# Cosine attention and a gated MLP in one kernel: loads, engine orders and the last store rearranged

## The chip, the cores and the metric

The kernel runs on one core of a Trainium2 chip. The metric is device time in microseconds (us) of one execution. A core has five engines that run at the same time, each with its own in-order list of instructions: TensorE (PE; its weight loads are shown as PEld), VectorE (DVE), ScalarE (ACT), GpSimd (POOL) and SyncE (SP). SP, ACT and POOL also issue DMA transfers from their lists. An instruction that waits for a semaphore holds back everything behind it on its engine.

## What is computed

For 8 batches of 12 heads (448 positions, 64 wide): rows of q and k are divided by their norms, the scores divided by tau = 0.1, softmax over the keys, and the product with v. The 12 heads' results side by side are the 3584 x 768 input of an MLP with 2048 hidden columns:

```python
q_n = q / (norm(q) + 1e-06);  k_n = k / (norm(k) + 1e-06)
scores = q_n @ k_n.T / tau
attn = exp(scores - max);  attn = attn / (sum(attn) + 1e-09)
x = (attn @ v)  # 12 heads side by side: [3584, 768]
h = x @ w_in
out = (h * cos(h)) @ w_out
```

## The kernel before

**Tiles.** Two pairs of heads make a "quad": 24 quads, three to a batch. A quad's Q and K (448 KB each) come through the SP queue (`load_one`, L394) into rings of three buffers Qf and Kf; its V comes through the POOL queue (`load_v`, L408) into a ring of four. W1 (the first MLP weight) is loaded in four pieces (`load_w1`, L416), W2 in four chunks (`load_w2`, L424), both on the POOL queue.

**A quad's work.** `square` (L434) squares Q and K on ScalarE or GpSimd, its `add` (L450) sums the squares on VectorE into n2; `inverse` (L458) makes 1/norm: a logarithm and an exponential on ScalarE, a sum with 1e-6 and a reciprocal on VectorE (quad 0: four ScalarE steps). `scale` (L489) multiplies, on VectorE or GpSimd, into Qn and Kn. They are transposed to qT and kT: quads 0 to 3 on TensorE (`transpose`, L510) with a copy from PSUM, later quads by DMA on the SP queue (`turn`, L527). `scores` (L539) is four matmuls into a pair of PSUM banks and one exponential E on ScalarE (L556), seven per quad; `attend` (L559) multiplies E with V. The softmax sums are made by matmuls with ones (`spread`, L579: quads 0 to 5; sums are inverted on ScalarE, L601 and L605) or with a selector (`sums` and `invert`, L622 and L638: later quads; a small store to DRAM from the ACT queue and a broadcast load R on the SP queue). The result goes into xT, by VectorE (L614, L617) or GpSimd (L657).

**The MLP.** For each batch c, a first stage of eight pairs of 12 matmuls (`m1_part`, L669, shown as L675), each pair followed on ScalarE and VectorE by four steps (`m1`: L688, L690, L692, L694) into gT; PSUM banks of a pair are reused after its L694. The second stage (`m2`, L697, shown as L703) makes 128 x 384 halves of a tile t of the output; a copy to osb (L711) follows on VectorE, and after the second half two stores of 64 rows on the SP queue (L717). `fill` cuts the second stage in pieces, and the lists VISITS and LATER (L723, L734) say how many of its matmuls stand between groups of three scores of the next batch's quads.

**Order.** A planner (L22) records operations with a cost and their dependencies. TensorE keeps the order of recording. Up to the line `P.strict = False` (L944) ScalarE, VectorE and GpSimd keep it too, through `behind` (L51); POOL's DMAs always do. After that, and for SP throughout, the planner picks by readiness and urgency in its own time model. So the start of the kernel (quads 0 to 2 and the norms of 3 and 4, L803 to L945) is an order written by hand. There, `gate` (L807) is the loads of quad 1: the first W1 piece waits for them. Quad 5's load waits for W2's chunk 2 (`half[3][:1]`, L895), quad 4's `turn` and quad 6's load for chunks 2 and 3. The copies of quad 3's transposes stand in the first MLP stage (L966).

Of the kernel before, what the change touches and what calls it, by code (L numbers as in the profile page):

```python
# [16 lines left out]
class Op:  # L17
    __slots__ = ("i", "eng", "dur", "fn", "reads", "writes", "deps", "dma", "lat", "start", "end",
                 "count", "waits", "known", "prio", "moves", "mode", "chain", "behind", "lead", "packet", "lock")


class Planner:  # L22
# [20 lines left out]
    def op(self, eng, dur, fn, r=(), w=(), after=(), dma=None, moves=0, mode="f", chain=None, keep=False, lead=0.0,  # L43
           packet=74, lock=False):
        o = Op()
        o.i, o.eng, o.dur, o.fn, o.dma, o.moves, o.mode, o.chain = (
            len(self.ops), eng, dur, fn, dma, moves, mode, chain)
        o.lat = self.FIRST + moves + self.LAST if dma else self.LAT[eng]
        o.behind, o.lead, o.packet, o.lock = None, lead, packet, lock
        if keep or self.strict and eng in ("act", "dve", "pool"):  # L50
            o.behind, self.tail[eng] = self.tail.get(eng), o  # L51
        o.reads, o.writes = tuple(r), tuple(w)
        deps = {a.i for a in after if a is not None}
        for x in o.reads:
            if x in self.last_write:
                deps.add(self.last_write[x].i)
        for x in o.writes:
            if x in self.last_write:
                deps.add(self.last_write[x].i)
            deps.update(p.i for p in self.readers.get(x, ()))  # L60
        deps.discard(o.i)
        o.deps = sorted(deps)
        for x in o.reads:
            self.readers.setdefault(x, []).append(o)
        for x in o.writes:
            self.last_write[x] = o
            self.readers[x] = []
        self.ops.append(o)
        return o
# [11 lines left out]

    PASSES, SPREAD = 0, 1.5

    def plan(self):

        rng = random.Random(1)
        shift = [0.0] * len(self.ops)
        least = max(o.end for o in self.pass_(shift))
        for _ in range(self.PASSES):
            n = rng.choice((8, 30, 100))  # L90
            i = rng.randrange(len(shift) - n)
            tried = list(shift)
            for k in range(i, i + n):
                tried[k] += rng.gauss(0.0, self.SPREAD)
            end = max(o.end for o in self.pass_(tried))
            if end <= least:
                least, shift = end, tried
        self.order = self.pass_(shift)
        return self.order

    def pass_(self, shift):
# [11 lines left out]
        t, urge = 0.0, [1e9] * len(ops)  # L113
        for o in ops:
            if o.eng == "pe":
                urge[o.i] = t
                t += o.dur
        later = None
        behind = {}
        for o in reversed(ops):  # L120
            if o.eng == "pe":
                if later is not None:
                    urge[o.i] = min(urge[o.i], urge[later.i] - o.dur)
                later = o
            if o.chain:
# [7 lines left out]
        for o in ops:  # L133
            o.prio = (urge[o.i] if urge[o.i] < 1e8 else 2000.0 + o.i) + shift[o.i] - o.lead
        pe = [o.i for o in ops if o.eng == "pe"]
        pe_next = 0
# [138 lines left out]
def bass_cosine_attention__then__act_gcu_kernel(  # L275
# [42 lines left out]
    sqk = sb("sqk", [128, 2 * NJ, D], BF16)  # L318
    n2 = ring("n2", 2, [128, 4 * NJ], F32)
    nrm = ring("nrm", 2, [128, 4 * NJ], F32)  # L320
    rr = ring("rr", 2, [128, 4 * NJ], F32)
    ne = ring("ne", 2, [128, 4 * NJ, 2], F32)
    Qn = ring("Qn", 1, [128, NJ, 2, D], BF16)
# [38 lines left out]
    for i in range(2):  # L362
        op("dve", 0.1, lambda e, i=i: e.memset(ne[i].ap()[:, :, 1], 1e-6), w=[("eps", i)])

# [65 lines left out]

    def jr(t, w, part, off=0):
        return bass.AP(t, off + w * H + part[0], [[2 * H, 128], [NJ, 2], [1, part[1] - part[0]]])

    def square(qd, w, eng, part=ALL[0], after=()):  # L434
# [15 lines left out]
        def add():  # L450
            return op("dve", 0.07 + 0.95 * n, lambda e: e.tensor_reduce(  # L451
                out=n2[u].ap()[:, H * w:H * w + H] if part == ALL[0] else jr(n2[u], w, part),
                in_=dst, axis=AX.X, op=ALU.add),
# [4 lines left out]
    def inverse(qd, w0, w1, part=ALL[0], after=()):  # L458
# [5 lines left out]
        if part == ALL[0]:  # L464
            n = slice(H * w0, H * w1)
            t, z, o = n2[u].ap()[:, n], nrm[u].ap()[:, n], rr[u].ap()[:, n]
        else:
            t, z, o = (jr(a[u], w0, part) for a in (n2, nrm, rr))
        act("exp", 0.12, lambda e: e.activation(z, t, ACT.Ln, bias=1e-30, scale=1.0),
# [3 lines left out]
        if qd == 0:  # L473
# [5 lines left out]
            return  # L479
        two_ = ne[u].ap()[:, H * w0:H * w1]  # L480
        act("exp", 0.12, lambda e: e.activation(two_[:, :, 0], z, ACT.Exp, bias=0.0, scale=0.5), r=x, w=[("ne", u)],
# [5 lines left out]
        op("dve", 0.3, lambda e: e.reciprocal(o, z), r=x, w=y, lead=lead)  # L487

    def scale(qd, w, eng="pool", part=ALL[0]):  # L489
        s, u = qd % 3, qd % 2  # L490
        j0, j1 = part
        f, n, nm = ((Qf, Qn, "Q"), (Kf, Kn, "K"))[w]
        rb = bass.AP(rr[u], w * H + j0, [[2 * H, 128], [NJ, 2], [1, j1 - j0], [0, D]])
        return op(eng, (1.05 if eng == "dve" else 1.65) * (j1 - j0) / NJ,
# [14 lines left out]

    def transpose(qd, which, bk, part=ALL[0]):  # L510
        u = qd % 3
# [3 lines left out]
        def mm(e):  # L515
# [122 lines left out]
    def invert(quads, bk):  # L638
# [8 lines left out]
        act("exp", 0.47, lambda e: e.activation(zz, zz, ACT.Exp, bias=0.0, scale=-1.0), r=[("Zs", z)], w=[("Zs", z)], lead=LEAD)  # L647
        op("act", 0.3, lambda e: e.dma_start(rscr.ap()[8 * n:8 * n + rows, :], Zs[z].ap()[0:32 * np_:16, :]),
           r=[("Zs", z)], w=[("rs", n)], dma=("rs", z), moves=0.05, lead=LEAD)
        for i, qd in enumerate(quads):  # L650
            u, sl, b = qd % 2, qd % NA, qd // QB
            for r in range(2):
                ap = bass.AP(rscr, (8 * n + 4 * i + 2 * r) * S, [[0, 64], [S, 2], [1, S]])
                op("sp", 0.6, lambda e, r=r, u=u, ap=ap: e.dma_start(R[u].ap()[64 * r:64 * r + 64], ap),
                   r=[("rs", n)], w=[("R", u, r)], dma=("R", u, r), moves=0.85, packet=140, lead=LEAD)
            c0 = 2 * (qd % QB)
# [40 lines left out]
    def m2(t, h, f0, f1, bk):  # L697
# [11 lines left out]
        if f1 == NNB:  # L709
            so = t % 3  # L710
            op("dve", 0.475, lambda e: e.tensor_copy(osb[so].ap()[:, HW * h:HW * h + HW], bank(bk, HW)),  # L711
               r=whole(bk), w=[("o", so, h)])
            if h:
                for sg in range(2):
                    b, cc = divmod(128 * t + 64 * sg, S)
                    dst = bass.AP(out.tensor, (S * b + cc // 64) * KM, [[NJ * KM, 64], [1, KM]])
                    op("sp", 0.6, lambda e, sg=sg, dst=dst: e.dma_start(dst, osb[so].ap()[64 * sg:64 * sg + 64, :]),  # L717
                       r=[("o", so, 0), ("o", so, 1)], w=[("out", t, sg)], dma=("store", so, sg), moves=0.55, packet=121)

# [3 lines left out]
    VISITS = [  # L723
# [7 lines left out]
        [],  # L731
        [],
    ]
    LATER = {19: 3, 10: -1, 18: -2, 5: 3, 4: 1, 17: 4, 7: -1, 21: -2, 22: -1, 15: -2, 9: 1}  # L734
    E1, E2 = NNB - 6, NNB - 4
# [69 lines left out]
    for part in HALVES:  # L805
        load_one(0, 1, part)
    gate = load_qk(1)  # L807
    load_qk(2)
# [25 lines left out]
    adds = [square(1, w, "act") for w in range(2)]  # L834
    adds[0]()
    load_qk(3)
# [3 lines left out]
    transpose(0, 1, 7, HALVES[1])  # L840
    adds[1]()
    for _ in inverse(1, 0, 2):
# [17 lines left out]
    spread(0, 4, 6)  # L860
    addk = square(2, 1, "act")
    addq = square(2, 0, "pool", after=[scaled])
# [85 lines left out]
    for c in range(B):  # L948
# [106 lines left out]
```

## Time and profile before

| what | value |
|---|---|
| median of three runs | 425.24 us (424.66 to 428.72) |
| the profiled execution | 424.88 us, its span 423.0 us |
| granted TensorE clock | 1.00 |
| first MLP stage begins (first L675) | 34.40 us |
| its second stage begins (first L703) | 54.48 us |
| second batch's first stage begins | 88.97 us |
| last copy ends | 419.35 us |

The span runs from the first to the last instruction; the rest of the time lies around it. A row of the timeline reads: start, duration, engine and line, operation, out<-in with shapes, and in brackets how long the engine had been idle and what ended that. Matmuls are pipelined, so TensorE's busy share includes some time that is not work at its peak. DMA issues are listed with the time from issue to landing.

### The profile page before, as it was taken

The numbers are of one execution on the slowest core, as the hardware profiler recorded it, in microseconds if no ns is written. First come the engines' busy times: TensorE is split into PE (matmuls) and PEld (weight loads), VectorE is DVE, ScalarE is ACT, GpSimd is POOL, SyncE is SP. The second block draws the span as 40 slices with busy tenths as digits, with TensorE's granted clock in tenths as the row PEclk, the third lists the DMA queues.
The fourth block names the chain that finished last, engine by engine and source line by source line (L and its number), as shares of the span: only waits on it lengthen the run. The fifth ranks groups of instructions, "written<-read, shape, count | busy, mean of one in ns | idle before, by whom it ended". The sixth has DMA issues, their size and how long they took to land.

```text
span 423.0 us, 8441 instructions
## 1 busy us (share of the span) xinstructions
PE 406.1 (96%) x3586; PEld 212.6 (50%) x3586; DVE 269.5 (64%) x337; ACT 306.3 (72%) x404; POOL 200.9 (47%) x137
## 2 busy tenths in 40 slices
PE   6879998999999999999999999999999999999995
PEld 5345454445544445445555555445554555555563
DVE  5767886879853659733996269824882228736921
ACT  6998689988888977697787677689678656505700
POOL 3566238792387794758628880559213213000000
PEclk9999999999999999999999999999999999999999
DMA  8999997995099969298909990279805523021022
GB/s 272 259 236 209 242 273 165 186 218 135 4 220 227 283 107 251 67 238 212 229 5 211 206 279 2 52 179 177 166 1 82 128 72 92 2 74 39 0 76 74
DMA packets 68230, 62.94 MB, mean 149 GB/s; under 512 B 39961, under 2 KB 60769, under 8 KB 68193
## 3 DMA queue, kind: packets, MB, share of 16 engines
q1 hardware_dynamic: 57808, 50.48, 48.3%
q0 software_dynamic: 10240, 11.80, 16.8%
q8 instruction: 28, 0.46, 0.5%
q10 hardware_dynamic: 144, 0.13, 0.1%
q14 instruction: 10, 0.07, 0.0%
HBM read 53.87 MB, written 11.14 MB: 154 GB/s over the span
## 4 chain that ended last, share of the span: by engine, by line
PE 77%; DMA 12%; ACT 4%; DVE 3%; POOL 2%; issue 0%; ACTq 0%; SPq 0%
PE PS L703 30%; PE PS L675 30%; PE PS L566 7%; PE PS L549 6%; DMA W<-in_moe_w_out_dram 6%; PE PS L629 3%; DMA Kf<-in_k_dram 3%; ACT E L556 2%; DMA R<-rscr 1%; DVE n L451 1%; PE PS L588 1%; DMA rscr<-Zs 1%; DMA Qf<-in_q_dram 1%; DVE osb L711 1%; POOL xT L657 0%
## 5 line engine op out<-in xcount | busy, mean ns | idle before, releaser
L556 ACT ACTIVATE E<-PS 128x896 bf16<-128x896 f32 x168 | 142.4, 919 | 20.8 <-PE PS L549 18.4
L703 PE MATMUL PS<-W,gT 128*128 128x384 bf16 x896 | 157.0, 327 | 0.0
L675 PE MATMUL PS<-xT,W 128*128 128x448 bf16 x768 | 147.0, 353 | 1.3 <-DVE qT L524 1.0
L703 PEld LDWEIGHTS PS<-W,gT 128*128 128x128 bf16 x896 | 82.9, 98 | 69.8 <-issue 15.9
L675 PEld LDWEIGHTS PS<-xT,W 128*128 128x128 bf16 x768 | 74.7, 98 | 71.7 <-DVE qT L524 1.1
L688 ACT ACTIVATE ar<-PS 128x896 int32<-128x896 f32 x64 | 58.2, 911 | 37.5 <-PE PS L675 37.5
L690 DVE SCALAR_TENSOR_TENSOR ar<-ar,PS 128x896 f32<-128x896 int32 x64 | 69.2, 1083 | 22.3 <-ACT ar L688 22.3
L694 DVE TENSOR_TENSOR gT<-PS,ar 128x896 bf16<-128x896 f32 x64 | 69.5, 1088 | 7.5 <-ACT ar L692 7.1
L692 ACT ACTIVATE ar<-ar 128x896 f32<-128x896 f32 x64 | 60.6, 946 | 18.2 <-DVE ar L690 18.0
L711 DVE COPY osb<-PS 128x384 f32<-128x384 f32 x56 | 31.1, 556 | 61.2 <-PE PS L703 60.5
L657 POOL TENSOR_TENSOR xT<-AVs,R 128x896 bf16<-128x896 f32 x18 | 37.4, 2086 | 49.6 <-DMA R<-rscr 49.6
L549 PE MATMUL PS<-qT,kT 64*64 64x448 bf16 x672 | 49.7, 359 | 5.3 <-ACT E L556 2.8
L447 POOL TENSOR_TENSOR sqq<-Qf 128x896 bf16<-128x896 f32 x22 | 36.9, 1677 | 34.0 <-DVE n L451 14.4
L447 POOL TENSOR_TENSOR sqk<-Kf 128x896 bf16<-128x896 f32 x21 | 36.9, 1756 | 33.2 <-DVE n L451 32.0
L495 POOL TENSOR_TENSOR Qn<-Qf,rr 128x896 bf16<-128x896 f32 x21 | 38.0, 1812 | 24.3 <-DVE rr L487 16.7
L575 DVE COPY AVs<-PS 128x896 f32<-128x896 f32 x21 | 22.8, 1088 | 29.2 <-PE PS L566 29.1
L566 PE MATMUL PS<-E,Vb 64*64 64x448 bf16 x672 | 36.7, 350 | 0.0
L451 DVE TENSOR_REDUCE n<-sqq 128x14 f32<-128x896 bf16 x24 | 25.7, 1072 | 14.3 <-POOL sqq L447 10.2
L549 PEld LDWEIGHTS PS<-qT,kT 64*64 64x64 bf16 x672 | 16.5, 105 | 31.8 <-ACT E L556 12.8
L495 POOL TENSOR_TENSOR Kn<-Kf,rr 128x896 bf16<-128x896 f32 x18 | 30.3, 1685 | 1.8 <-DMA kT<-Kn 1.8
L451 DVE TENSOR_REDUCE n<-sqk 128x14 f32<-128x896 bf16 (+2 forms) x25 | 25.9, 1040 | 5.8 <-POOL sqk L447 5.8
L566 PEld LDWEIGHTS PS<-E,Vb 64*64 64x64 bf16 x672 | 18.8, 107 | 12.7 <-issue 1.9
(45 smaller groups left out, 175.7 us busy)
## 6 DMA issues: line engine op xcount, KB each, us to landing
Qf<-in_q_dram SPq DMA_DIRECT2D x24, 448.0 KB, 5.4
out_dram<-osb SPq DMA_DIRECT2D x56, 192.0 KB, 3.6
Kf<-in_k_dram SPq DMA_DIRECT2D x23, 448.0 KB, 5.9
R<-rscr SPq DMA_DIRECT2D x36, 224.0 KB, 4.5
Vb<-in_v_dram POOLq DMA_DIRECT2D x24, 224.0 KB, 5.7
W<-in_moe_w_in_dram POOLq DMA_DIRECT2D x4, 768.0 KB, 17.7
W<-in_moe_w_out_dram POOLq DMA_DIRECT2D x4, 768.0 KB, 24.4
qT<-Qn SPq DMA_TRANSPOSE x20, 4.1
```

What stands on the lines that cost most here:

```text
L447: op(eng, (1.68 if eng == "pool" else 1.05) * n, lambda e: e.tensor_tensor(dst, src, src, ALU.mult), r=cut(nm + "f", s, part), w=cut("sq" ...
L451: return op("dve", 0.07 + 0.95 * n, lambda e: e.tensor_reduce(out=n2[u].ap()[:, H * w:H * w + H] if part == ALL[0] else jr(n2[u], w, part) ...
L495: lambda e: e.tensor_tensor(n[0].ap()[:, j0:j1].rearrange("p j r d -> p r j d"), f[s].ap()[:, :, j0:j1], rb, ALU.mult),
L549: ins = e.matmul(bank(bs + r, S, 64 * a, 64 * a + 64), kT[u].ap()[64 * r:64 * r + 64, j, a, :], qT[u].ap()[64 * r:64 * r + 64, :, a, :], s ...
L556: act("exp", 0.81, lambda e: e.activation(E[es].ap(), two(bs), ACT.Exp, bias=0.0, scale=INV_TAU), r=pair(bs), w=[("E", es)], chain="E")
L566: ins = e.matmul(bank(bk + a, S, 64 * r, 64 * r + 64), Vb[vs].ap()[64 * a:64 * a + 64, r, j, :], E[es].ap()[64 * a:64 * a + 64, r, :], sta ...
L675: ins = e.matmul(bank(bk + i2), W1.ap()[:, i, 128 * nb:128 * nb + 128], xT[c % 2].ap()[:, i, :], start=(i == 0), stop=(i == NKC - 1))
L688: op("act", 0.815, lambda e: e.activation(ar[s].ap().bitcast(I32), two(bk), ACT.Identity, bias=0.25, scale=INV2PI), r=bs, w=[("ar", s)])
L690: op("dve", 1.005, lambda e: e.scalar_tensor_tensor(ar[s].ap(), ar[s].ap().bitcast(I32), -2.0 * math.pi, two(bk), ALU.mult, ALU.add), r=bs ...
L692: act("sin", 0.86, lambda e: e.activation(ar[s].ap(), ar[s].ap(), ACT.Sin, bias=GUARD * math.pi / 2.0, scale=GUARD), r=[("ar", s)], w=[("a ...
L694: op("dve", 1.01, lambda e: e.tensor_tensor(gT.ap()[:, 2 * pr:2 * pr + 2, col:col + S], two(bk), ar[s].ap(), ALU.mult), r=bs + [("ar", s)] ...
L703: ins = e.matmul(bank(bk, HW), gT.ap()[:, f, col:col + 128], W2.ap()[:, f, HW * h:HW * h + HW], start=(f == 0), stop=(f == NNB - 1))
```

## The change

1. Quad 1's loads wait until quad 0's Q has landed (`load_qk(1, [first])`); quad 2's loads are as before.
2. Each recorded operation gets a key: its number, plus an entry of a table MOVE while `strict` holds. TensorE's list and the strict lists of ScalarE, VectorE, GpSimd and POOL's DMAs are sorted by that key. The random passes of the planner, which were set to none, are gone.
3. The square of quad 2's K moves from ScalarE to GpSimd and is recorded earlier; the squares of quad 1 change places.
4. n2, nrm, rr and ne become one tile each with both buffers; a function `inverse_two` is added, which would make the norms of two quads at once. Nothing calls it.
5. The copies of quad 3's transposes go to ScalarE (`eng="act"`).
6. The planner's costs of the softmax sums' store and broadcast load are raised; VISITS and LATER have new numbers.
7. The last tile's halves are stored each as soon as it is copied, 64 rows from the SP queue and 64 from the ACT queue.

```diff
+        o.key = o.i + (self.MOVE.get(o.i, 0) if self.strict else 0)
         if keep or self.strict and eng in ("act", "dve", "pool"):
-            o.behind, self.tail[eng] = self.tail.get(eng), o
+            self.tail.setdefault(eng, []).append(o)
...
+    MOVE = {50: -10.0, 101: -3.5, 179: -5.0, 83: -3.0, 19: -7.0, 124: -2.5, 94: 0.0, 187: -5.0, 204: 9.0, 123: 9.0,
...
+            140: 5.5, 51: 2.5}
...
+        for line in self.tail.values():
+            line.sort(key=lambda o: o.key)
+            for a, b in zip(line, line[1:]):
+                b.behind = a
...
+        pe = [o.i for o in sorted((o for o in ops if o.eng == "pe"), key=lambda o: o.key)]
...
+        if eng == "act":
+            op("act", 0.13 + 0.067 * (j1 - j0), lambda e: e.activation(dst, src, ACT.Copy), r=whole(bk), w=cut(nm + "T", u, part))
+            return
...
+            if end:
+                store(t, HW * h, HW * h + HW, [("o", so, h)], ("sp", "act"))
+            elif h:
+                store(t, 0, KM, [("o", so, 0), ("o", so, 1)])
...
-        [(0, 25), (3, 12), (3, 11), (3, 6), (3, 0), (3, 10), (3, 12), (3, 5), (3, 5), (3, 0), (3, 4), (3, 4), (1, 1)],
+        [(0, 25), (3, 12), (3, 11), (3, 4), (3, 4), (3, 11), (3, 10), (3, 4), (3, 5), (3, 0), (3, 4), (3, 6), (1, 0)],
...
-    gate = load_qk(1)
+    gate = load_qk(1, [first])
...
     adds = [square(1, w, "act") for w in range(2)]
-    adds[0]()
+    adds[1]()
     load_qk(3)
...
-    adds[1]()
+    adds[0]()
+    addk = square(2, 1, "pool")
...
-    addk = square(2, 1, "act")
...
-                    transpose(FIRST, w, at_bank[pr] + w)
+                    transpose(FIRST, w, at_bank[pr] + w, eng="act")
```

The lists that come of it, up to the first MLP stage, differ in these places (old order, then new):

- SP: Q0, K0, Q1, K1, K2, Q2; now Q0, K0, Q2, K2, (wait for Q0) K1, Q1. Later: quad 7's loads ahead of quad 5's; now quad 5's ahead of quad 7's.
- POOL: V0, V1, two pieces of W1, V2, two of W1, square of quad 2's Q, V3, W2 chunks 0 1 2 3; now V0, V2, V1, three pieces of W1 (first half, second half, first half of the columns), square of quad 2's K, the fourth piece, W2 chunk 2, square of quad 2's Q, chunks 1 3 0, V3.
- ScalarE: the first logarithm of quad 0 ahead of the square of K's second part; quad 1's K squared ahead of its Q; the square of quad 2's K gone; in the first MLP stage the two copies behind L688 of pair 2, and L692 of pair 2 ahead of that of pair 1.
- VectorE: quad 1's sums (K first) ahead of quad 0's last copy; quad 1's last scale ahead of its first copy; quad 2's K sum ahead of quad 1's last copy; quad 2's last copy ahead of quad 0's xT; quad 3's K sum ahead of quad 1's xT; in the first MLP stage the sum of quad 5's Q behind L690 of pair 3 (before: behind the stage).
- TensorE: scores and attends of quads 0 to 2 change places at four points, and five fill-in matmuls stand behind a transpose instead of ahead of it.

More of the change, by code (lines that the diff above doesn't have):

```diff
@@ L18 @@
     __slots__ = ("i", "eng", "dur", "fn", "reads", "writes", "deps", "dma", "lat", "start", "end",
-                 "count", "waits", "known", "prio", "moves", "mode", "chain", "behind", "lead", "packet", "lock")
+                 "count", "waits", "known", "prio", "moves", "mode", "chain", "behind", "lead", "packet", "lock", "key")
 class Planner:
@@ L80, in land @@
         return s + took + self.LAST
-    PASSES, SPREAD = 0, 1.5
-    def plan(self):
[L86 to L98, printed above, removed]
+    MOVE = {50: -10.0, 101: -3.5, 179: -5.0, 83: -3.0, 19: -7.0, 124: -2.5, 94: 0.0, 187: -5.0, 204: 9.0, 123: 9.0,
[7 rows of a table added]
+    def plan(self):
+        for line in self.tail.values():
+            line.sort(key=lambda o: o.key)
+            for a, b in zip(line, line[1:]):
+                b.behind = a
+        self.order = self.pass_([0.0] * len(self.ops))
         return self.order
@@ L113, in pass_ @@
         t, urge = 0.0, [1e9] * len(ops)
[L114 to L118, printed above, removed]
+        pe = [o.i for o in sorted((o for o in ops if o.eng == "pe"), key=lambda o: o.key)]
+        for i in pe:
+            urge[i] = t
+            t += ops[i].dur
+        later = dict(zip(pe, pe[1:]))
         behind = {}
         for o in reversed(ops):
[L121 to L124, printed above, removed]
+            if o.i in later:
+                urge[o.i] = min(urge[o.i], urge[later[o.i]] - o.dur)
             if o.chain:
@@ L134, in pass_ @@
             o.prio = (urge[o.i] if urge[o.i] < 1e8 else 2000.0 + o.i) + shift[o.i] - o.lead
-        pe = [o.i for o in ops if o.eng == "pe"]
         pe_next = 0
@@ L487, in inverse, with inverse_two @@
         op("dve", 0.3, lambda e: e.reciprocal(o, z), r=x, w=y, lead=lead)
+    def inverse_two():
+        flat = "p u n -> p (u n)"
+        t, z, o = (a.ap().rearrange(flat) for a in (n2, nrm, rr))
+        c2, x, y = ([c for u in range(2) for w in range(2) for c in cut("%s%d" % (k, w), u, ALL[0])] for k in ("n2", "nrm", "rr"))
+        both = ne.ap().rearrange("p u n i -> p (u n) i")
+        act("exp", 0.17, lambda e: e.activation(z, t, ACT.Ln, bias=1e-30, scale=1.0), r=c2, w=x)
+        act("exp", 0.17, lambda e: e.activation(both[:, :, 0], z, ACT.Exp, bias=0.0, scale=0.5), r=x,
+            w=[("ne", 0), ("ne", 1)])
+        op("dve", 0.2, lambda e: e.tensor_reduce(out=z, in_=both, axis=AX.X, op=ALU.add),
+           r=[(k, u) for k in ("ne", "eps") for u in range(2)], w=x)
+        op("dve", 0.55, lambda e: e.reciprocal(o, z), r=x, w=y)
     def scale(qd, w, eng="pool", part=ALL[0]):
@@ L508, in norm_b, with transpose @@
         return last
-    def transpose(qd, which, bk, part=ALL[0]):
+    def transpose(qd, which, bk, part=ALL[0], eng="dve"):
         u = qd % 3
@@ L710, in m2, with store @@
             so = t % 3
+            end = t == B * S // 128 - 1
             op("dve", 0.475, lambda e: e.tensor_copy(osb[so].ap()[:, HW * h:HW * h + HW], bank(bk, HW)),
                r=whole(bk), w=[("o", so, h)])
[L713 to L718, printed above, removed]
+            if end:
+                store(t, HW * h, HW * h + HW, [("o", so, h)], ("sp", "act"))
+            elif h:
+                store(t, 0, KM, [("o", so, 0), ("o", so, 1)])
+    def store(t, x0, x1, parts, engs=("sp", "sp")):
+        so = t % 3
+        for sg, eng in enumerate(engs):
+            b, cc = divmod(128 * t + 64 * sg, S)
+            dst = bass.AP(out.tensor, (S * b + cc // 64) * KM + x0, [[NJ * KM, 64], [1, x1 - x0]])
+            src = osb[so].ap()[64 * sg:64 * sg + 64, x0:x1]
+            op(eng, 0.6, lambda e, dst=dst, src=src: e.dma_start(dst, src), r=parts, w=[("out", t, sg, x0)],
+               dma=("store", so, sg, x0), moves=0.55 * (x1 - x0) / KM, packet=121)
     QUADS = [4, 5, 3, 3, 3, 3, 0, 0]
```

32 lines of the change are left out of this document (16 added, 16 removed), and 18 rows, old and new, of tables (MOVE, VISITS).

## The prediction

> **What bounds the kernel now.** I read the page's busy line first, then the chain of waits, then busy time by stretches, then the start and the end of the timeline. TensorE is busy 406.1 of 423.0 us. The chain of waits runs through TensorE almost without a break from 89 us on, and the number of matmuls stays. What can move is the start, the few gaps, and the tail.
>
> ```profile
> PE 406.1 (96%) x3586; PEld 212.6 (50%) x3586; DVE 269.5 (64%) x337; ACT 306.3 (72%) x404; POOL 200.9 (47%) x137
> ```
> Busy time by stretches (columns: PE, PEld, DVE, ACT, POOL, clock, DMA share, GB/s): from 10 to 40 us ScalarE is the full engine, not TensorE, and the DMA engines are full too.
> ```profile
> 10.00:20.00 10.00, 7.79 (x118) 3.74 (x122) 8.19 (x15) 9.09 (x13) 5.21 (x7) 1.00 1.14 259
> 20.00:30.00 10.00, 8.16 (x142) 4.63 (x134) 6.82 (x11) 9.94 (x15) 6.88 (x7) 1.00 1.12 242
> 62.00:89.00 27.00, 25.10 (x325) 12.23 (x317) 21.11 (x26) 25.86 (x38) 22.25 (x13) 1.00 0.89 182
> ```
> The timeline of the start: the squares of quad 1 on ScalarE, then E0 (in-order behind them), then E2, which opens the full stretch; quad 2's K square sits inside it.
> ```profile
> 9.60 0.93 ACT L444 ACTIVATE sqk<-Kf 128x896 bf16<-128x896 f32 x1
> 11.21 1.73 ACT L556 ACTIVATE E<-PS 128x896 bf16<-128x896 f32 x2 [0.68 <-PE PS L549]
> 13.44 4.33 ACT L556 ACTIVATE E<-PS 128x896 bf16<-128x896 f32 x5
> 17.67 0.94 ACT L444 ACTIVATE sqk<-Kf 128x896 bf16<-128x896 f32 x1
> 18.51 1.72 ACT L556 ACTIVATE E<-PS 128x896 bf16<-128x896 f32 x2
> ```
> DMA issues of the seventh load of the start (here Q of quad 2, issued at 3.80): 8.7 us to landing. Then three waits of the second MLP stage's stretch, and the last store.
> ```profile
> Qf<-in_q_dram SPq DMA_DIRECT2D x1, 448.0 KB, 8.7
> 62.46 0.23 ACT L469 ACTIVATE nrm<-n 128x28 f32<-128x28 f32 x1 [0.83 <-DVE n L451]
> 71.08 0.38 PE L549 MATMUL PS<-qT,kT 64*64 64x448 bf16 x4 [0.82 <-DVE AVs L575]
> 82.76 1.52 PE L588 MATMUL PS<-E,ones 64*64 64x448 bf16 x28 [0.57 <-ACT E L556]
> 419.38 1.10 SPq L717 DMA_DIRECT2D out_dram<-osb  x2
> ```
>
> **The change, part by part.** The profiled execution took 424.88 us, 0.36 under the median of 425.24; its span is 423.0. The sum is made on the 424.88.
>
> *Norms in one.* `inverse_two` is defined and called nowhere: the norms of quads 3 and 4 stay as they are. Price 0. The one-tile layout of n2, nrm, rr and ne changes addresses alone.
>
> *First loads.* Quad 1's loads now wait for Q of quad 0; quad 2's do not. So the SP queue issues Q0, K0 (two parts), Q2, K2, then waits until Q0 lands (0.74 + 3.6 = 4.34) and issues K1 and Q1. Quad 0 is followed as closely as before, so its landings stay; quad 1 falls from places four and five to six and seven. Landings before: place four 2.27+5.5 = 7.8, five 2.78+6.2 = 9.0, six 10.2, seven 3.80+8.7 = 12.5. I take Q1 at 12.5, as the same V loads compete with it (V of quad 0 landed at 12.7, the second V at 13.5). Q1's square on ScalarE, now second, starts at 12.55, E0 0.84 later (spacing 9.60-8.76) at 13.39, E2 2.23 after that (13.44-11.21): 15.62 against 13.44, **+2.18**. Bounds: at the pace of the loads before it (1.2 apart) Q1 lands at 11.4, +1.1; at the second V's 13.5, +3.2. ScalarE is full from there to the first MLP stage, so this passes on. The small reorder in quad 0's norm (a logarithm ahead of K's second square) costs under 0.1 and ends before quad 1 lands: 0.
>
> *K square of quad 2 to GpSimd.* It leaves ScalarE's full stretch: 18.51-17.67, **-0.84**. On GpSimd it stands after the third W1 issue: 12.55 + three issues (1.33+0.68) = 14.6, and 1.68 long: ends 16.3. VectorE sums it after quad 1's copies, near 19; hidden by E2 to E6 (five of 0.86). E7 needs quad 1's first K copy: K's second scale (0.55) now stands before the Q copy, yet the copy ends near 17.72+2.18-0.42 = 19.5, and ScalarE comes free at 19.9: 0.
>
> *VectorE, TensorE and GpSimd orders to 34 us.* The sums of quads 3 and 4 keep their producers' order, V of quads 1 and 2 swap, attends move between scores: all lie beside ScalarE, busy 9.94 of 10. Price 0; if ScalarE were not full they would cost at most the 0.8 that TensorE waited at 31.39.
>
> *Copies of quad 3's transposes to ScalarE.* TensorE waited 0.96 at 43.12 for VectorE's copy (42.46, 0.61 long, behind a gT). ScalarE's free slot follows its own L688 at 42.34, and a 128x896 pass takes it about 0.9: ends 43.15, no gain. VectorE is spared 1.22, but a sum of quad 5 (1.08) comes into this stage. I take **+0.1**, between -0.96 (the wait gone) and +0.6 (2x0.92 against 1.22).
>
> *POOL queue: W2 order and V3.* W2 goes out as chunks 2, 1, 3, 0, V of quad 3 after them. Quad 5's load hangs on chunk 2: the third chunk landed at 47.2 (21.36+25.86), the first at 39.8. W1's first issue waits for quad 1 (9.3 becomes 12.55), but the DMA engines have other work (share 1.14), so I take 39.8 less V3's place (0.8 between the landings at 35.2 and 36.0): 39.0, at most 39.0+3.3 = 42.3. Quad 5's Q then lands at 39.0+8.5 (row of the load at 43.57) = 47.5, its square ends 49.2; the sum's slot on VectorE is about 49.6 (47.7+1.34+0.5). No wait. Behind that sum stand L690 and gT of pairs 3 to 7, and ScalarE and TensorE wait for those. Chunk 0, wanted first by the second matmul, is now last: chunks took 3.7 us alone and 6.2 beside other loads, so it lands between 39.0+3x3.7 = 50.1 and, with loads beside it after 1.5 us, 39.0+1.5+9.6x(6.2/3.7) = 56.6, against a start at 54.48+1.4 = 55.9. Taken **+0.3**, bounds 0 and +4.0 (42.3 instead of 39.0).
>
> *Stage cuts (VISITS, LATER), 58 to 89 us.* Quad 5's norm comes earlier, so ScalarE's 0.83 goes, and with it TensorE's 0.43 at 65.42; four m2 matmuls (0.65) now stand behind quad 3's attend and cover most of the 0.82 at 71.08. TensorE idles 1.9 there. Taken **-0.9**, bounds -1.9 and +0.8 (a new wait such as that 0.82).
>
> *107 to 346 us.* Idle of TensorE is 1.25 in all. The tightest return trip, quad 8's sums to its xT, has one matmul (0.16) less cover and was 0.3 late: **+0.1**, bounds -1.25 and +1.5 (as much again lost).
>
> *Tail.* Now: copy ends 419.35, two stores issue in 1.10, the second lands 419.92+2.6. After: the first half goes early, and two half-size stores issue side by side. Issue saves 0.54; the transfer window, 420.7 to 422.2 for both, shrinks by a part of its 1.5. Taken **-0.8**, bounds -1.1 and -0.5. The Trainium skill (DMA: Bandwidth & Descriptors, Rules for kernel authors) speaks against more: spreading stores over queues only saves the issue time; by it alone the term would be -0.54 and the sum 0.26 higher. No run here yet shows a split store.
>
> Sum: +2.18 -0.84 +0.1 +0.3 -0.9 +0.1 -0.8 = **+0.14**, so 424.88+0.14 = **425.0**.
>
> **The rivals.**
> *Late weights (slower).* If the W1 wait is not covered, chunk 2 lands at 42.3: quad 5's square ends 52.5, VectorE waits 2.9 inside the first MLP stage with everything behind it; chunk 0 lands up to 4.0 late. Some 3.3 instead of 0.3: 428.0. It decides from chunk 2 landing at 39.4. For: quad 5's square waited 11.8 for its load before. Against: the DMA share.
> *Port held.* GpSimd's square meets VectorE's scale of quad 1 (16.36): with TENSOR_TENSOR on both, VectorE's took 2.30 instead of 1.09 at 86.78, while GpSimd's had begun at 86.46. If the square starts 0.5 later than worked out, quad 1's chain loses 1.2: 426.2. The Trainium skill (SBUF — State Buffer, Who interferes with whom) says the two engines can lock each other out of a shared port for a whole instruction; the 2.30 at 86.78 agrees. Against: the square ends at 16.3, just before.
> *Quad 1 at the old pace.* Q1 lands at 11.4: 1.1 less, 423.9. For: 1.2 between places five and six. Against: 2.3 between six and seven.
> *Gaps close.* The 1.9 of 58 to 89 and the 1.25 later all go: -1.0 and -1.35 on the sum, 422.6. Against: ScalarE is busy 25.86 of 27 there.
>
> **How the numbers follow.** Chances: forecast 0.45 (own range 424 to 426.5), late weights 0.18, quad 1 at the old pace 0.15, gaps close 0.12, port held 0.10. The two gains together with the low tail reach 421.2; late weights with Q1 at 13.5 reach 428.9 and beyond. Range 422.3 to 429.0. A measurement of this kernel tells about 1% (4.25 us) from no change: faster by that 0.04 (both gains and more), slower 0.10 (the upper half of late weights), same 0.86.
>
> **What would show it.** E2 near 15.6 and the first L675 near 35.7 (34.40 before): first term. No ScalarE square between E6 and E7: second. GpSimd's square of quad 5 before 49 and no wait on VectorE's n at L447: weights. First L703 near 55.9, not waiting for W. No 0.83 before the norm near 62. Last copy to the end 2.85 us instead of 3.65. Wrong if E2 is under 14.5, if VectorE waits over 1 us in the first MLP stage, or if a new TensorE gap over 1 us stands after 107.

## The result, and the profile after

The changed kernel is slower by about half a per cent: a median of 428.29 us (427.07 to 433.12, 22 runs) against 426.51 us (424.34 to 431.2, 22 runs), ratio 1.0048 with a 95% interval of 1.0025 to 1.0070. The forecast was 425.0, and no change. Of the 3.3 us that the median lies above it, 1.6 come of its base: the sum was made on one execution of 424.88, and the kernel before has a median of 426.51. The profiled execution took 427.46 us with a span of 425.6 (before: 424.88 and 423.0). Ratios below are to the kernel before, with their intervals. Line numbers have moved: L444 is L440, L495 is L504, L549 is L561, L556 is L568, L675 is L687, L703 is L715.

The busy line of the page, where TensorE's share of the span is what it was:
```profile
PE 408.0 (96%) x3586; PEld 213.7 (50%) x3586; DVE 268.9 (63%) x335; ACT 307.7 (72%) x405; POOL 202.7 (48%) x138
```
Busy time by stretches, as before (PE, PEld, DVE, ACT, POOL, clock, DMA share, GB/s):
```profile
10.00:20.00 10.00, 5.24 (x58) 2.36 (x59) 5.97 (x10) 6.02 (x9) 5.08 (x6) 0.66 1.12 244
20.00:30.00 10.00, 8.27 (x124) 4.54 (x125) 7.36 (x14) 9.91 (x15) 6.15 (x7) 1.00 1.10 242
62.00:89.00 27.00, 26.42 (x336) 12.53 (x334) 20.42 (x27) 26.48 (x38) 19.74 (x12) 1.00 0.82 191
```
From 10 to 20 us ScalarE, which was the full engine there (9.09), now works 6.02, TensorE falls from 7.79 to 5.24, and the granted clock is 0.66. From 62 to 89 TensorE has gained 1.3 (the same window holds work that lies 3.6 us earlier in this kernel). The timeline of the start, ScalarE and one row of TensorE:
```profile
11.53 0.95 ACT L440 ACTIVATE sqk<-Kf 128x896 bf16<-128x896 f32 x1 [2.85 <-DMA Kf<-in_k_dram]
...
13.93 0.95 ACT L440 ACTIVATE sqq<-Qf 128x896 bf16<-128x896 f32 x1 [1.45 <-DMA Qf<-in_q_dram]
...
14.79 1.71 ACT L568 ACTIVATE E<-PS 128x896 bf16<-128x896 f32 x2
...
15.74 0.59 PE L561 MATMUL PS<-qT,kT 64*64 64x448 bf16 x4 [3.81 <-ACT E L568]
...
16.77 0.90 ACT L568 ACTIVATE E<-PS 128x896 bf16<-128x896 f32 x1
...
18.02 0.92 ACT L568 ACTIVATE E<-PS 128x896 bf16<-128x896 f32 x1 [0.35 <-PE PS L561]
...
19.56 0.92 ACT L568 ACTIVATE E<-PS 128x896 bf16<-128x896 f32 x1 [0.62 <-PE PS L561]
```
The brackets are the story: ScalarE stands still 2.85 us for quad 1's K and 1.45 for its Q. E0, whose scores have been ready since 11.2, stands behind both squares and runs 3.58 late (14.79; 11.21 before), E2 3.33 late. TensorE idles 3.81 us for it, and then four matmuls take 0.59 us instead of 0.38, so that ScalarE waits twice for scores, 0.97 in all. The granted clock (the last column but two) goes with it:
```profile
12.00:14.00 2.00, 0.00 (x0) 0.00 (x0) 1.08 (x1) 0.55 (x2) 0.00 (x0) 0.69 1.18 267
14.00:16.00 2.00, 0.26 (x4) 0.13 (x4) 1.09 (x2) 2.00 (x3) 1.80 (x3) 0.50 1.12 330
16.00:18.00 2.00, 1.69 (x18) 0.53 (x15) 1.29 (x4) 1.64 (x4) 2.00 (x3) 0.50 1.02 180
18.00:20.00 2.00, 2.00 (x23) 0.93 (x24) 1.93 (x3) 1.35 (x2) 1.28 (x2) 0.60 1.09 203
```
The load behind it, among the DMA issues (KB, us from issue to landing), issued at 4.60, so landed at 13.9:
```profile
Qf<-in_q_dram SPq DMA_DIRECT2D x1, 448.0 KB, 9.3
```
Later in the timeline: the norm of quad 5 no longer waits, quad 8's xT comes late, and the last store. Before, TensorE waited 0.33 us for that xT:
```profile
149.63 16.82 PE L675 MATMUL PS<-xT,W 128*128 128x448 bf16 x88 [0.33 <-POOL xT L657]
```
After:
```profile
64.41 0.23 ACT L465 ACTIVATE nrm<-n 128x28 f32<-128x28 f32 x1
...
153.66 16.82 PE L687 MATMUL PS<-xT,W 128*128 128x448 bf16 x88 [1.33 <-POOL xT L669]
...
420.12 3.11 ACTq L737 DMA_DIRECT2D out_dram<-osb  x2
...
422.13 0.56 DVE L724 COPY osb<-PS 128x384 f32<-128x384 f32 x1 [2.04 <-PE PS L715]
```
Where the 2.6 us of span are, stage by stage. A stage begins where the row of its first matmul starts, so the second batch's begins at 88.81 before; at 88.97, the time given above, the row ahead of it ends.

| stretch | before, us | after, us | difference | forecast |
|---|---|---|---|---|
| to the first MLP stage | 34.40 | 38.02 | +3.62 | +1.34 |
| to its second stage | 20.08 | 20.16 | +0.08 | +0.4 |
| to the second batch's first stage | 34.33 | 33.13 | -1.20 | -0.9 |
| to the seventh batch's first stage | 256.99 | 257.83 | +0.84 | +0.1 |
| to the last copy's start | 72.99 | 72.99 | 0 | 0 |
| to the end of the span | 4.21 | 3.47 | -0.74 | -0.8 |

### The profile page after: what moved, and what is told of

The parts are those of the page before. It is cut to its first block, busy times and chain, and to the rows that moved or that the text cites. A ratio compares the mean times of both kernels' runs of the same rounds, so it can differ in the third digit from the quotient of the medians.

```text
span 425.6 us, 8454 instructions
## 1 busy us (share of the span) xinstructions
PE 408.0 (96%) x3586; PEld 213.7 (50%) x3586; DVE 268.9 (63%) x335; ACT 307.7 (72%) x405; POOL 202.7 (48%) x138
## 4 chain that ended last, share of the span: by engine, by line
PE 85%; ACT 6%; DMA 5%; DVE 1%; POOL 0%; issue 0%; ACTq 0%; SPq 0%
PE PS L687 33%; PE PS L715 33%; PE PS L561 7%; PE PS L578 7%; ACT E L568 4%; DMA Qf<-in_q_dram 3%; PE PS L641 3%; PE PS L600 2%; DMA R<-rscr 1%; DMA rscr<-Zs 1%; DVE osb L724 1%; POOL xT L669 0%; ACT ar L700 0%; ACT ar L617 0%; ACT ar L613 0%
## 5 line engine op out<-in xcount | busy, mean ns | idle before, releaser
L568 ACT ACTIVATE E<-PS 128x896 bf16<-128x896 f32 x168 | 142.9, 917 | 24.4 <-PE PS L561 20.7
L715 PE MATMUL PS<-W,gT 128*128 128x384 bf16 x896 | 156.8, 327 | 0.0
L687 PE MATMUL PS<-xT,W 128*128 128x448 bf16 x768 | 147.0, 353 | 2.4 <-POOL xT L669 1.3
L715 PEld LDWEIGHTS PS<-W,gT 128*128 128x128 bf16 x896 | 83.0, 98 | 69.7 <-issue 16.9
L687 PEld LDWEIGHTS PS<-xT,W 128*128 128x128 bf16 x768 | 74.5, 98 | 73.0 <-POOL xT L669 1.8
L706 DVE TENSOR_TENSOR gT<-PS,ar 128x896 bf16<-128x896 f32 x64 | 69.4, 1088 | 7.8 <-ACT ar L704 7.4
L704 ACT ACTIVATE ar<-ar 128x896 f32<-128x896 f32 x64 | 60.5, 947 | 15.6 <-DVE ar L702 15.2
L561 PE MATMUL PS<-qT,kT 64*64 64x448 bf16 x672 | 50.0, 363 | 6.8 <-ACT E L568 5.8
L504 POOL TENSOR_TENSOR Qn<-Qf,rr 128x896 bf16<-128x896 f32 x21 | 38.1, 1814 | 36.7 <-DVE rr L483 28.1
L443 POOL TENSOR_TENSOR sqk<-Kf 128x896 bf16<-128x896 f32 x22 | 38.6, 1754 | 28.9 <-DVE n L447 26.5
L561 PEld LDWEIGHTS PS<-qT,kT 64*64 64x64 bf16 x672 | 16.7, 106 | 33.0 <-issue 13.4
L504 POOL TENSOR_TENSOR Kn<-Kf,rr 128x896 bf16<-128x896 f32 x18 | 30.4, 1688 | 3.1 <-DMA kT<-Kn 3.0
```

What stands on the lines that cost most here:

```text
L443: op(eng, (1.68 if eng == "pool" else 1.05) * n, lambda e: e.tensor_tensor(dst, src, src, ALU.mult), r=cut(nm + "f", s, part), w=cut("sq" ...
L504: lambda e: e.tensor_tensor(n[0].ap()[:, j0:j1].rearrange("p j r d -> p r j d"), f[s].ap()[:, :, j0:j1], rb, ALU.mult),
L561: ins = e.matmul(bank(bs + r, S, 64 * a, 64 * a + 64), kT[u].ap()[64 * r:64 * r + 64, j, a, :], qT[u].ap()[64 * r:64 * r + 64, :, a, :], s ...
L568: act("exp", 0.81, lambda e: e.activation(E[es].ap(), two(bs), ACT.Exp, bias=0.0, scale=INV_TAU), r=pair(bs), w=[("E", es)], chain="E")
L687: ins = e.matmul(bank(bk + i2), W1.ap()[:, i, 128 * nb:128 * nb + 128], xT[c % 2].ap()[:, i, :], start=(i == 0), stop=(i == NKC - 1))
L704: act("sin", 0.86, lambda e: e.activation(ar[s].ap(), ar[s].ap(), ACT.Sin, bias=GUARD * math.pi / 2.0, scale=GUARD), r=[("ar", s)], w=[("a ...
```

## The experiments

Theory: quad 1's loads, gated and put behind quad 2's, are the loss; the clock that falls while TensorE waits adds to it; the rest of the change pays back some. Rivals: the clock is harmless, or the loss is in the queue orders, the copies and the cuts.

**1. Quad 1's loads not gated.**
```diff
-    gate = load_qk(1, [first])
+    gate = load_qk(1)
```


> The kernel after, with quad 1's loads no longer waiting for Q of quad 0; all the rest of the change stays. Main theory (the wait for the first load, put on quad 1 and not on quad 2, makes ScalarE's E0 late, and all that follows): Q of quad 1 lands near 8 us again, E0 near 11.2 (14.79 after), E2 near 13.4, the granted clock is 1.0 from 10 us on, the first MLP stage starts near 33.6 (38.02 after; 34.40 before less the 0.84 of the K square that went to GpSimd), and the total is about 4 us under the kernel after, 1 to 2 us under the kernel before. Rival (the time is lost elsewhere: order of W2, the copies on ScalarE, the stage cuts): the first MLP stage starts earlier but the total stays within 1 us of the kernel after.

Measured: 424.17 us, ratio 0.9964 (0.9930 to 0.9998): 0.84% under the kernel after, and under the kernel before. The gate's loss is all of it and more.
```profile
11.11 1.73 ACT L568 ACTIVATE E<-PS 128x896 bf16<-128x896 f32 x2 [0.72 <-PE PS L561]
...
13.56 1.68 POOL L443 TENSOR_TENSOR sqk<-Kf 128x896 bf16<-128x896 f32 x1 [2.01 <-DVE nrm L480]
...
13.85 2.34 DVE L504 TENSOR_TENSOR Qn<-Qf,rr 128x896 bf16<-128x896 f32 x1
...
17.61 1.92 ACT L568 ACTIVATE E<-PS 128x896 bf16<-128x896 f32 x2 [1.18 <-PE PS L561]
```
E0 is back at 11.11, the clock at 1.00. But the first MLP stage starts at 34.49, not at 33.6: GpSimd's square meets VectorE's scale, which takes 2.34 instead of 1.09, and ScalarE waits 1.18 at 17.61.

**2. Both quads gated**, so quad 1 is ahead of quad 2 again, but behind the wait.
```diff
-    load_qk(2)
+    load_qk(2, [first])
```


> The kernel after, with quad 2's loads waiting for Q of quad 0 as well, so that quad 1's loads stand ahead of quad 2's again, but all behind the wait. If the lost time is the swapped order (quad 1 behind quad 2), Q of quad 1 lands near 9 to 10 us, before quad 0's chain needs ScalarE, E0 is near 11.5 and the total lies 3 to 4 us under the kernel after. If it is the wait itself (queue left empty until 4.3 us), Q of quad 1 lands at 11 or later, E0 at 12.5 or later, and less than half of the 4 us comes back.

Measured: 425.39 us, 0.9991 (0.9965 to 1.0016).
```profile
9.57 0.93 ACT L440 ACTIVATE sqq<-Qf 128x896 bf16<-128x896 f32 x1
...
11.21 1.73 ACT L568 ACTIVATE E<-PS 128x896 bf16<-128x896 f32 x2 [0.71 <-PE PS L561]
```
The total is 2.4 us under the kernel after (3 to 4 were expected), and the first MLP stage starts at 34.82. Q's square runs at 9.57 without waiting for its load, E0 at 11.21: it is the place behind quad 2, not the wait as such, that costs. The two runs without and with the wait (0.9964 and 0.9991) overlap.

**3. TensorE kept busy.** 64 more fill-in matmuls.
```diff
-    warm(8, Y)
+    warm(72, Y)
```


> The kernel after, with 72 fill-in matmuls instead of 8 ahead of the first scores, into a scratch bank that nothing reads, so that TensorE does not stand idle for 3.81 us before 15.74. If the idle time costs by itself, through the granted clock of 0.5 to 0.6 from 14 to 20 us: E0 stays near 14.8 and E2 near 16.8, the matmul groups at L561 take 0.38 again instead of 0.59, ScalarE's waits of 0.35 and 0.62 for PS go, and the first MLP stage starts near 37.0 instead of 38.02, the total about 1 us lower. Rival (the late landing of quad 1's loads is all of it, the slow matmuls are hidden behind ScalarE): first MLP stage within 0.3 us of 38.02 and the same total.

Measured: 426.40 us, 1.0006 (0.9984 to 1.0028), so 1.8 us less than the kernel after (0.42% of 428).
```profile
14.45 1.71 ACT L568 ACTIVATE E<-PS 128x896 bf16<-128x896 f32 x2
...
15.49 0.38 PE L561 MATMUL PS<-qT,kT 64*64 64x448 bf16 x4
...
16.43 3.32 ACT L568 ACTIVATE E<-PS 128x896 bf16<-128x896 f32 x4
```
E0 stays late (14.45), the matmuls take 0.38 again, ScalarE's four exponentials run without a gap. From E2 to the first MLP stage it is 20.38 us instead of 21.25, and that stage starts at 36.81: the clock alone cost 0.9 there. Where the rest of the 1.8 comes from was not traced. (In its profiled execution quad 8's wait was 1.65, so that one shows less of the gain than the median.)

**4. The gate alone, on the kernel before.**
```diff
-    gate = load_qk(1)
+    gate = load_qk(1, [first])
```


> The kernel before, with nothing changed but that quad 1's loads wait for Q of quad 0. Main theory: this alone loses more than the whole change does, since nothing pays it back: E0 3.3 to 3.6 us later than 11.21, the granted clock under 0.7 near 16 us, the first MLP stage 3.3 to 4.5 us after 34.40, and the total 3 to 4.5 us over the kernel before. Rival (the loss is in the other parts): the total within 1.5 us of the kernel before.

Measured: 428.95 us, 1.0073 (1.0045 to 1.0102). The first MLP stage starts at 38.20, 3.80 late, with the same pattern:
```profile
13.16 0.95 ACT L444 ACTIVATE sqk<-Kf 128x896 bf16<-128x896 f32 x1 [1.43 <-DMA Kf<-in_k_dram]
...
14.02 1.71 ACT L556 ACTIVATE E<-PS 128x896 bf16<-128x896 f32 x2
...
14.97 0.59 PE L549 MATMUL PS<-qT,kT 64*64 64x448 bf16 x4 [3.03 <-ACT E L556]
```
So this one wait loses about as much as the whole change, or more (the two intervals overlap). This kernel also has the old cuts and still waits 1.35 us for quad 8's xT.

**5 and 6. The K square: out of VectorE's way, or back on ScalarE**, both on experiment 1. In 5 K of quad 2 is loaded ahead of its Q (`lead`, a new argument of `load_one`, makes a load more urgent to the planner); in 6 the square stands between E6 and E7 again (its entry in MOVE becomes 28.5).
```diff
-    load_qk(2)
+    load_one(2, 0)
+    load_one(2, 1, lead=3.0)
```
```diff
-    addk = square(2, 1, "pool")
+    addk = square(2, 1, "act")
```


> The kernel of the first experiment (quad 1's loads not waiting), and in it K of quad 2 loaded ahead of Q of quad 2, so that GpSimd can square it before VectorE scales quad 1. There GpSimd's square at 13.56 met VectorE's scale at 13.85, which took 2.34 us instead of 1.09, and ScalarE then waited 1.18 at 17.61. Theory (the two engines hold each other up; the square's gain of 0.84 was eaten by that): K of quad 2 lands near 10.2 to 11, the square ends by 13.5, the scale takes 1.1 again, ScalarE's wait at 17.61 is under 0.4, the first MLP stage starts at 33.4 to 33.8 instead of 34.49, and the total is 0.7 to 1.0 us under that experiment's. Rival (moving the square off ScalarE gains nothing, since something else is full there): the scale takes 1.1, and the first MLP stage still starts at 34.3 or later.

> The kernel of the first experiment (quad 1's loads not waiting), with the K square of quad 2 back on ScalarE, between E6 and E7, as before. Theory (hold-up): the scale of quad 1 on VectorE takes 1.09, no wait of 1.18 on ScalarE, the square's 0.84 is back on it; the first MLP stage starts at 34.2 to 34.6, as without this edit, so the move to GpSimd was worth 0 there, and the total is within 0.5 us of the first experiment's. Rival (the move was worth its 0.84 and the first experiment lost it to something else): the first MLP stage at 35.0 or later.

Measured: 5 starts the first MLP stage at 33.38, 6 at 34.24, experiment 1 at 34.49. Here is 5:
```profile
11.79 1.68 POOL L443 TENSOR_TENSOR sqk<-Kf 128x896 bf16<-128x896 f32 x1 [1.46 <-DVE n L447]
...
13.20 6.04 ACT L568 ACTIVATE E<-PS 128x896 bf16<-128x896 f32 x7
...
13.94 1.09 DVE L504 TENSOR_TENSOR Qn<-Qf,rr 128x896 bf16<-128x896 f32 x1
```
The square ends before the scale begins, the scale takes 1.09, seven exponentials run without a gap. The move, with K loaded sooner, is worth 0.86 (34.24 less 33.38) where the two engines don't meet; where they do, experiment 1 starts no sooner than 6. Yet 5 took 427.40 us (1.0031, 0.9998 to 1.0063) and 6 only 424.34 (0.9966, 0.9937 to 0.9994). The total expected of 5 was wrong. Its profiled execution, which took 429.85, shows where it went:
```profile
153.15 19.73 PE L687 MATMUL PS<-xT,W 128*128 128x448 bf16 x88 [3.44 <-POOL xT L669]
```
TensorE waited 3.44 for quad 8's xT, and the 88 matmuls behind it took 19.73 instead of 16.82, with the clock at 0.50 from 153 to 159. Against the 1.1 us won at the start stands a loss of 6.3 in this execution (3.44, and 19.73 less 16.82). That the earlier start made that wait longer is not shown.

**7. The last tile's store alone, on the kernel before** (the `store` function of the change and its call).

> The kernel before, with the last tile's store alone cut as in the change (each half column-wise as it is ready, from SP's and ScalarE's queues). Forecast term -0.8, and the kernel after showed 2.9 us from the last copy to the end instead of 3.65: the last copy stays within 0.1 us of its place apart from waits that vary by themselves, the tail is 2.85 to 2.95, and the total 0.5 to 0.9 us lower. Rival (the early half's stores delay the others, or only the issue time of 0.54 is saved): a tail of 3.1 or more.

Measured: 425.14 us, 0.9988 (0.9962 to 1.0014): too small for the time to tell. The profile tells: from the last copy's start (421.09) to the end of the span it is 3.5 us, as in the kernel after (3.47), against 4.21 before. That fits the term, at -0.7.

**8. The K square alone on GpSimd, on the kernel before.**
```diff
+    addk = square(2, 1, "pool")
```
(behind quad 1's squares, in place of the one on ScalarE)

> The kernel before, with the K square of quad 2 alone moved to GpSimd, early in its queue, as in the change. K of quad 2 lands at 10.2 here, GpSimd's issues end at 12.7, so the square stands at about 12.7 to 14.4, and VectorE scales from 14.18. Theory (the square's 0.84 is real where it does not meet the scale): the scale takes at most 1.4, E7 comes 0.5 to 0.84 earlier, the first MLP stage starts at 33.6 to 33.9 (34.40 before), the total is 0.4 to 0.9 us lower. Rival (it meets the scale anyway or nothing is gained): first MLP stage at 34.3 or later.

Measured: 426.82 us, 1.0013 (0.9985 to 1.0041), first MLP stage at 34.84: the rival held.
```profile
13.45 1.73 POOL L447 TENSOR_TENSOR sqk<-Kf 128x896 bf16<-128x896 f32 x1
...
14.27 1.87 DVE L495 TENSOR_TENSOR Qn<-Qf,rr 128x896 bf16<-128x896 f32 x1
...
17.56 0.92 ACT L556 ACTIVATE E<-PS 128x896 bf16<-128x896 f32 x1 [0.71 <-PE PS L549]
```
The square starts 0.75 later than worked out and meets the scale (1.87).

**9 and 10. More work beside quad 8's trip**, on 5 and on 6: in the second list of VISITS `(0, 21)` becomes `(0, 15)` and the last `(1, 0)` becomes `(1, 6)`.

> The kernel of the fifth experiment (quad 1's loads not waiting, K of quad 2 sooner), whose first MLP stage began at 33.38, with six matmuls of the second batch's second MLP stage moved from ahead of its first scores to behind its last ones. In that experiment TensorE waited 3.44 us at 153.15 for quad 8's xT (the sums' store and broadcast load took 5.29 and 7.20 us), and the clock then fell for some 3 us. Theory (that wait is a return trip with too little work beside it, and the clock follows the idle time): six matmuls are 0.98 us more cover, so the wait shrinks by about 1.0 for a trip of the same length, seldom reaches the length after which the clock falls, and the total goes 1 to 3 us under the fifth experiment's, to 424 to 426. Rival (the early start itself moves the transfers into each other's way, and the trip grows with it): the wait at quad 8's xT stays over 2.5 us and the total over 426.5.

> The kernel of the sixth experiment (quad 1's loads not waiting, K square of quad 2 on ScalarE) with the same six matmuls moved behind the second batch's last scores. Its wait at quad 8's xT was 0.91 with a trip of 10.56 us from the store's issue to xT. Theory: with 0.98 more cover the wait is 0 for a trip of up to about 10.6, and the total 0.3 to 0.9 us lower than the sixth experiment's, the best so far; rival (the six matmuls were needed ahead of the first scores, where ScalarE now falls behind): a new wait of TensorE for E or PS of 0.5 us or more near 110 to 130, and no gain.

Measured: 430.50 us (1.0106, 1.0067 to 1.0145) and 431.12 us (1.0130, 1.0094 to 1.0166). Neither theory nor rival: quad 8's wait is gone, and a new one, earlier, is worse. The chain of waits of 10 (start, us, what):
```profile
122.36 6.83 DMA rscr<-Zs
...
129.21 0.49 SPq L666
...
129.74 0.60 SPq L666
...
130.38 1.54 SPq L666
...
131.96 0.60 SPq L666
...
132.60 4.81 DMA kT<-Kn
...
137.46 0.58 PE PS L561
```
The planner answered the six matmuls with another order of SP's queue. A transpose kT now stands behind the four loads of R (L666), which wait for the store of sums (6.83 us here); TensorE stood still 4.20 us (2.40 in 9), and the clock fell again.

**11. The old cuts, on experiment 6** (VISITS and LATER of the kernel before).

> The kernel of the sixth experiment with VISITS and LATER as in the kernel before. Forecast for the cuts: -0.9 between 58 and 89 and +0.1 behind 107. From the runs so far (first stage of the first batch to that of the second 53.3 to 54.3 with the new cuts; the cover of quad 8's trip 9.64 with the new, 10.11 with the old cuts): a wait of 0.8 for AVs near 71 comes back and TensorE loses 0.4 to 0.9 there, quad 8's wait is 0.47 shorter for the same trip, and the total is within 0.6 us of the sixth experiment's. Rival (the cuts are what makes that kernel faster than the one before): the total 1 us or more higher.

Measured: 428.30 us, 1.0063 (1.0032 to 1.0094): 1% over experiment 6, the rival. Again a queue:
```profile
127.53 4.04 DMA R<-rscr
...
131.65 2.08 POOL xT L669
...
134.58 2.10 POOL xT L669
136.68 1.56 POOL Qn L504
...
138.29 1.69 POOL Kn L504
...
140.00 2.96 DMA kT<-Kn
...
143.05 0.59 PE PS L561 x3
```
GpSimd's scale of a quad stands behind two xT that wait for R; TensorE waited 2.56. The wait of 0.82 near 71 came back too, as forecast. In the kernel before, with the same cuts, that scale stands ahead of the two xT; so the order comes of the old cuts together with something else of the change. The planner's new costs are a candidate, and were not tried by themselves.

**12. W2's order alone, on the kernel before.**
```diff
-    half[2] += [load_w2(f, ()) for f in range(2)]
-    half[3] += [load_w2(f, ()) for f in range(2, 4)]
+    w2 = {f: load_w2(f, ()) for f in (2, 1, 3, 0)}
+    half[2] += [w2[0], w2[1]]
+    half[3] += [w2[2], w2[3]]
```


> The kernel before, with W2's chunks alone issued in the order 2, 1, 3, 0 of the change, so that quad 5's load, which waits for chunk 2, goes out some 7 us sooner. In three profiles of kernels with the old order ScalarE waited 0.83, 2.54 and 2.48 us near 62 to 65 for the norm of quad 5, and TensorE lost 0.43, 2.13 and 2.08 near 66. Theory (the order removes a wait that the first profile showed at its shortest): no wait of ScalarE for that norm, none of TensorE near 66, first MLP stage of the second batch 53.6 to 54.0 us after that of the first (54.4, 56.1 and 56.1), and the total 0.5 to 2 us lower than before. Rival (chunk 0, wanted first, is then late): TensorE waits for W at its first second-stage matmuls near 55, by 0.5 us or more.

Measured: 427.85 us, 1.0025 (0.9993 to 1.0057). The wait near 66 is gone, as expected, and a new one stands earlier:
```profile
49.28 1.08 DVE L451 TENSOR_REDUCE n<-sqq 128x14 f32<-128x896 bf16 x1 [1.72 <-POOL sqq L447]
...
56.12 4.22 PE L703 MATMUL PS<-W,gT 128*128 128x384 bf16 x25 [1.60 <-DVE gT L694]
...
62.31 0.23 ACT L469 ACTIVATE nrm<-n 128x28 f32<-128x28 f32 x1
```
VectorE stood 1.72 us for the square of quad 5, with the next gT behind that sum, and TensorE then 1.60 for gT, not for W. This is the late-weights rival's mechanism, at half its price, and the second batch's first stage came 55.5 us after the first batch's, not 53.6 to 54.0. In the kernel after it did not happen: its first stage began 3.6 us later than before, and the square, at 48.77, came 10.8 us after that start (here, at 47.56, 13.3 us). Why the median is 2.6 us above the profiled execution (425.29) is open; the seven executions of 427.68 and more had a mean granted clock of 0.993 to 0.997, the other five 0.998 to 1.000, which points to half clock, as behind a TensorE gap, in most of the seven.

## Why the prediction was wrong

*First loads: the step that failed.* It took quad 1's Q to land at 12.5, because the seventh load of the kernel before landed there. But the seventh issue now waits for quad 0 and goes out at 4.60 instead of 3.80, and took 9.3 us instead of 8.7: landed 13.9, beyond the upper bound of 13.5. E2 was 3.33 late, not 2.18. Of the 2.46 us that the span gained beyond the forecast, 2.28 lie in this stretch. Experiments 1 and 4 give the whole step as 0.84% and 0.73%, 3.1 to 3.6 us with what hangs on it.

*A term that was missing: the clock.* I worked out that E0 would be late and never asked what TensorE does meanwhile. It idled 3.81 us and ran at half clock until 19.6; ScalarE waited 0.97 for scores. Experiment 3 prices this at 0.9 us in that stretch, 1.8 in the median. With E2 at 3.33 and the clock at 0.97, less 0.84 for the K square, the start comes to +3.46 of the +3.62 found. The remaining 0.16 may lie in the orders that were priced at 0; they were not tried by themselves.

*K square: right by luck.* As far as that sum tells, -0.84 held in the kernel after, because the late loads put the scale (17.51) behind most of the square (16.19 to 17.90): it took 1.35. The square itself began at 16.19, not at 14.6. The rival "port held" is what the move does without the gate (1, 2, 8), unless K is loaded sooner (5). The Trainium skill (SBUF — State Buffer, Who interferes with whom) has the two engines lock each other out of a shared port; the rows agree: 2.34 and 1.87 where they meet, 1.09 where not.

*Copies on ScalarE, W2's order.* +0.1 and +0.3 against +0.08 for the stage; weights were not late. The two terms were not tried apart in this kernel; TensorE's wait for quad 3's copy is 1.03 (46.82) against 0.96. The margin worked out for quad 5's sum (0.4 us) was real, and experiment 12 shows it used up.

*58 to 89.* -1.20 against -0.9, in the range. The norm's wait is gone. It had been shown at its shortest: 0.83 in the profile before, 2.54 and 2.48 in experiments 7 and 8, which have the same order.

*107 to 346: mis-sized, +0.84 against +0.1.* It is quad 8's trip, +1.00; the other gaps of the stretch are 0.16 shorter. The trip runs from the issue of the store of sums to the start of xT. Less the cover (TensorE's work meanwhile, without the 2.1 us that xT itself takes), it gives the wait in each of these profiles, or none where the cover is longer: the cover is 10.11 with the old cuts and 9.64 with the new, a loss of 0.47 (0.16 forecast). The trip itself varies:

| kernel | trip, us | cover | wait |
|---|---|---|---|
| before | 137.05 to 147.49: 10.44 | 10.11 | 0.33 |
| experiment 4 | 140.19 to 151.67: 11.48 | 10.11 | 1.35 |
| after | 140.56 to 151.53: 10.97 | 9.64 | 1.33 |
| experiment 2 | 138.18 to 148.40: 10.22 | 9.64 | 0.58 |
| experiment 1 | 138.02 to 149.49: 11.47 | 9.64 | 1.82 |
| experiment 5 | 137.93 to 151.02: 13.09 | 9.64 | 3.44 |
| experiment 8 | 139.15 to 148.34: 9.19 | 10.11 | 0 |
| experiment 12 | 138.01 to 147.14: 9.13 | 10.11 | 0 |

So about half of the 1.00 between 1.33 and 0.33 is the change (0.47), and half how this execution's transfers fell (0.53); one profile could not tell.

*Tail: right*, -0.74 against -0.8, more than the -0.54 that saving the issue time alone would give. The sign named for it, the last copy to the end, held.

The rivals: late weights did not come, nor the old pace, nor closing gaps; the port held VectorE's scale by 0.26 (1.35 against 1.09). None of them was the case that came, a later landing with a cold TensorE behind it. The range held the result by 0.7 us, but for other reasons than the ones it was built on. Of the three signs that the forecast named against itself, the TensorE gap after 107 came (1.33). VectorE's wait of over 1 us came too (1.29 at 48.45, for ScalarE's L704), but it tells nothing: the kernel before has 1.08 and 1.02 in the same stage.

## What to carry to other kernels

When one load is made to wait, look at what is issued instead of it, which engine's in-order list meets its landing first, and what stands behind that on the list. When TensorE will idle for more than about 2 us (here the line lay between 1.82 and 2.40), price the clock as well, or fill the gap. A gain of a microsecond early moves the transfers behind it: check the tightest return trip by its cover, and do not read one execution's trip as its length.

## What the runs showed of the hardware

- Between 8 us and the last matmul, the granted clock fell to 0.50 around every TensorE gap of 2.40 us or more that the profiles hold (2.40, 2.56, 3.03, 3.44, 3.81, 4.20), and stayed at 1.00 around gaps of 1.82 and less. It stayed down for about 3.4 or 6.8 us: 136.6 to 140.0 in 9, 143.0 to 146.4 in 11, 12.8 to 19.6 in the kernel after, 152.2 to 159.1 in 5. The fall does not follow from the gap's length alone: in the kernel after it came 0.8 us into a gap that began at 11.93, in 9 1.0 us after the gap had ended. The two windows of 9:
```profile
136.00:138.00 2.00, 2.00 (x36) 0.85 (x28) 0.00 (x0) 1.73 (x2) 2.00 (x2) 0.66 1.05 381
...
140.00:142.00 2.00, 2.00 (x14) 1.18 (x13) 0.00 (x0) 1.62 (x3) 2.00 (x3) 0.99 0.84 136
```
  At 0.66 over 2 us, half clock lasted 1.36 us of the first; TensorE had been at work again since 135.65. The Trainium skill (TensorE: Matmul & The Clock Gate, What's actually happening) has the clock halved after an idle window of some 3.4 us in a free-running count; the lengths agree with such a window, but gaps of 2.40 and 2.56 us were enough here.
- A DMA round trip of the same bytes at the same place (14 KB out, four loads of 224 KB back, up to the start of the multiplication that waits for them) took 9.1 to 13.1 us in the eight kernels of the table.
- GpSimd's square and VectorE's scale (a TENSOR_TENSOR whose inputs both lie in SBUF) at the same time: the later one is held until the earlier is done. In experiments 1 and 8 and the kernel after the scale ended 0.95 to 0.96 us after the square (in 1 it ran from 13.85 to 16.19, and the square ended at 15.24); a scale alone takes 1.09. A TENSOR_TENSOR with one input in PSUM was not held (gT at L706, 48.45 in the kernel after: two in 2.09 beside the square of 48.77), and a TENSOR_REDUCE beside GpSimd's square kept its 1.08 (51.45 there, beside the square of 50.62).
